# Order of the down-projection and the plan of weight rounding in a fused attention and feed-forward kernel

## The chip, the cores and the metric

The kernel runs on one core of a Trainium2 chip. The metric is the device time of one execution in microseconds (us), lower is better. The core has a matmul engine (TensorE, PE in the profile; PEld are its weight loads), a vector engine (VectorE, DVE), a scalar engine (ScalarE, ACT), GpSimd (POOL) and SyncE (SP), which issues most of the transfers. Each engine works through its own list of instructions.

## The reference, cut to what matters

Clustered attention feeds a feed-forward block. A query attends only to those keys that were given the same cluster code (16 clusters, the code is the argmax of the similarity to normalised centroids).

```python
q_assign = argmax(einsum(q_n, c_n)); k_assign = argmax(einsum(k_n, c_n))
scores = where(q_assign == k_assign, q @ k.T / sqrt(64), -1e9)
attn = softmax(scores)
x = (attn @ v), heads side by side        # (4 * 768, 8 * 64)
h = x @ w_in                              # (3072, 2048)
g = h - tanh(h)
out = g @ w_out                           # (3072, 512)
```

There are 4 batches, 8 heads, 768 tokens and a head size of 64. The feed-forward weights come as 64-bit floats.

## The kernel before

**Attention.** Two heads at a time make a pair; a batch has 4 pairs (`HP`), so there are 16. A pair's work is cut into steps: two halves of the queries (384 tokens each, `TB`), and in each half three steps (`NS`) of two key blocks. `steps` is the list of all of them; the first 12 (`HALF`) are the first half of the queries of pairs 0 to 3, the next 12 their second half, and then the pairs follow one by one. In every step a Python loop records, in this order:

- the stage `similar` (L319) of a later pair, if it is due
- `begin` of the next step: the score matmuls (L419, `sc`), and for the first halves of pairs 1 to 3 the masking matmuls with the one-hot tile `hot` (L430); then ScalarE's exponential (L441)
- `rest_of` of up to two of the weight pieces that the step is to round (L140, ScalarE)
- `value` of this step: the matmuls with v (L473) into `av`, of which there is one accumulator; in masked halves also the sums (L482, `den`)
- at the end of a half `take`, ScalarE's copy of `av` to `xT` (L492), which frees the accumulator
- the filling items of the step (the feed-forward of the batch before), and between them `todo`: the selects of the next step (L451, VectorE), `one_hot` (L394, L398), `publish` (the codes: L364, the cast `qc` of L368, a transfer to memory), `spread_both` (the broadcast load of `hot`, L386), `route` (L338 to L345), the chain that inverts the softmax sums (`total` L505, `compact` L522, `invert` L528, `spread_out` L535, `scale` L541; or `divide` L546, L549), and the rounding of the pieces.

The order on each engine is the order in which the loop records, so an instruction that waits holds up what is recorded behind it on its engine.

**Rounding.** The 64-bit weights are cut into 32 pieces of 512 KB, 16 of `w_in` and then 16 of `w_out`, each in the order of quarters 0, 2, 1, 3 (`ORDER`). A piece is loaded into one of three buffers `raw` (L193, issued by GpSimd). ScalarE turns the low words into `rest` (two buffers, L140), and VectorE makes the rounded value with three instructions (L145, L149, L152). Only when a piece is done is the load of the third next one issued (`AHEAD` = 3). Two pieces are rounded before the loop; `paces` says how many each step takes after that. Between one step and the next nothing else paces them.

**Filling.** In steps 12 to 23 the items of `plain_items(0)` fill TensorE: 16 items `up` (h = x @ w_in, L568; tanh on ScalarE, L573; g = h - tanh on VectorE, L575), then 12 items `project` (L584). A `project` item adds one quarter of `w_out` (four pieces) to the output of one block of 128 tokens; a half has three blocks (`HCH`) and four quarters (`NQ4`). The finished block is copied by ScalarE (L592) into a tile that shares its buffers with `rest`, and stored by GpSimd's queue (L593). `plain_items(1)` fills steps 24 to 47; from the second batch on another algorithm with seven products (L758, L806) takes over. The tiles `h`, `o`, `sim`, `pr`, `pq` and `den` in the accumulator memory share one pool of three buffers (`ps_f`); the scores have two buffers (`ps_s`).

Of the kernel before, what the change touches and what calls it, by code (L numbers as in the profile page):

```python
# [57 lines left out]
def kernel(  # L58
# [24 lines left out]
    HCH = NCH // 2  # L83
    NQ4 = 4
# [69 lines left out]
    def fast():  # L154
# [402 lines left out]
        def plain_items(half: int):  # L557
            gs, acc = {}, {}
            sequence = [i * FQ + o for i in ORDER for o in range(FQ)]

            def up(f: int, between):
                i, o = f // FQ, f % FQ
                if f < CF // 2:
                    gs[f] = gp.tile([P, 2, TB], F32, name="g")
                h = ps_f.tile([P, TB], F32, name="h", tag="f")
                for c in range(CD):
                    for r in halves:
                        nc.tensor.matmul(  # L568
                            h[r], lhsT=w_in[i][:, c, o * P : (o + 1) * P][:, r], rhs=xT[c][:, half],
                            start=(c == 0), stop=(c == CD - 1),  # L570
                        )
                th = thp.tile([P, TB], F32, name="th")
                nc.scalar.activation(out=th, in_=h, func=ACT.Tanh)  # L573
                between()
                nc.vector.tensor_tensor(  # L575
                    out=gs[f % HF][:, f // HF], in0=h, in1=th, op=ALU.subtract
                )

            def project(sub: int, i: int, between):
                if i == 0:  # L580
                    acc[sub] = ps_f.tile([P, DM], F32, name="o", tag="f")
                for f in sequence[i * FQ : (i + 1) * FQ]:
                    for r in halves:
                        nc.tensor.matmul(  # L584
                            acc[sub][r], lhsT=gs[f % HF][:, f // HF, sub * P : (sub + 1) * P][:, r],
                            rhs=w_out[f // FQ][:, f % FQ],
                            start=(f == sequence[0]), stop=(f == sequence[-1]),
                        )
                between()
                if i == NQ4 - 1:  # L590
                    osb = restp.tile([P, DM], F32, name="osb", tag="rest")
                    nc.scalar.copy(out=osb, in_=acc.pop(sub))  # L592
                    nc.gpsimd.dma_start(out_r[0, half * HCH + sub], osb)  # L593


            return [(2.6, 1, lambda between, f=f: up(f, between)) for f in sequence] + [
                (3.4, 1, lambda between, s=s, i=i: project(s, i, between))
                for s in range(HCH) for i in range(NQ4)
            ]


# [249 lines left out]
        NS = NCH // 2  # L851
        HALF = HP * NS
# [116 lines left out]


        fills = {HALF: (lambda: plain_items(0), HALF), 2 * HALF: (lambda: plain_items(1), 2 * HALF)}
        for b in range(1, B - 1):
            fills[2 * (b + 1) * HALF] = (lambda b=b: strassen_items(b), 2 * HALF)


        paces = {at: 1 + at % 2 for at in range(NS, HALF)}
        paces.update({at: 3 if 13 < at < 17 else 2 for at in range(HALF, HALF + 7)})
        late, divides, makers, later = [], [], [], {}
        fill, whole, spent, since, over = [], 0.0, 0.0, 0, 1
        for at, (n, half, s) in enumerate(steps):  # L980
# [72 lines left out]
            def between():  # L1053
                i = next(place)
                for it in todo[i * len(todo) // slots : (i + 1) * len(todo) // slots]:
                    it()

                if i == turned_at and 0 in stages:
                    stages[0]()
# [190 lines left out]
    with ExitStack() as cx, tc.manual_schedule():  # L1250
        fast()
# [35 lines left out]
```

## Time and profile before

| | |
|---|---|
| time, median of 3 | 1020.6 us (1019.93 to 1020.68) |
| profiled span | 1017.8 us, mean granted TensorE clock 0.996 |
| PE busy | 989.5 us (97%) |
| DVE busy | 553.0 us (54%) |
| ACT busy | 297.6 us (29%) |
| POOL busy | 500.1 us (49%) |
| h matmuls, L568 | 512 records, 488 ns in the mean |
| o matmuls, L584 | 384 records, 593 ns in the mean |
| loads of raw pieces | 16 + 16 of 512 KB, 4.9 and 4.5 us to landing in the median |

A row of a timeline gives the start in us, the length in us, the engine, the line, the operation, the tile written and those read, their sizes, and the number of instructions merged. The bracket at its end tells how long the engine was idle before it and what released it. Matmul records overlap, and a float32 matmul leaves two records, so the length of a merged row divided by its number is what one record adds to the time. One item `up` is 16 records, one item `project` too.

### The profile page before, as it was taken

What the parts mean: (1) busy time and instruction counts of PE and PEld (TensorE: products, weight loads), DVE (VectorE), ACT (ScalarE), POOL (GpSimd) and SP (SyncE); (2) the same over time, 40 slices, a digit from 0 to 9 for tenths busy, and PEclk for the clock granted to TensorE, in tenths of its full rate; (3) what the DMA queues carried; (4) which work ended last, traced back from release to release, by engine and by line L of the source; (5) the groups of instructions that cost most, each with busy time, mean ns of one, the idle gap of its engine ahead of it and who ended that gap; (6) DMA issues with size and microseconds to landing.
All of it is one profiled execution on the core that took longest, in us unless ns stands there. A gap on an engine that the chain in (4) does not pass through costs nothing.

```text
span 1017.8 us, 16547 instructions
## 1 busy us (share of the span) xinstructions
PE 989.5 (97%) x6444; PEld 471.4 (46%) x6444; DVE 553.0 (54%) x1047; ACT 297.6 (29%) x458; POOL 500.1 (49%) x343
## 2 busy tenths in 40 slices
PE   8998898999999999999999999999999999999997
PEld 4433343334443334444455555444445555344665
DVE  6468895446675657656545347755645336544011
ACT  4453443223333323332331212233332221122000
POOL 1013443345434455666678244566679345465600
PEclk9998999999999999999999999999999999999999
DMA  7654452022744834344455556344442332333321
GB/s 219 172 148 145 134 164 74 31 57 70 188 140 129 264 119 130 114 138 139 155 160 176 162 153 174 128 163 120 145 161 79 110 107 66 106 109 116 109 94 39
DMA packets 115681, 132.46 MB, mean 130 GB/s; under 512 B 62688, under 2 KB 95372, under 8 KB 112908
## 3 DMA queue, kind: packets, MB, share of 16 engines
q1 hardware_dynamic: 109212, 109.80, 35.4%
q0 software_dynamic: 6240, 21.50, 6.3%
q8 instruction: 53, 0.87, 0.4%
q14 instruction: 32, 0.26, 0.1%
q10 hardware_dynamic: 144, 0.03, 0.0%
HBM read 110.14 MB, written 21.17 MB: 129 GB/s over the span
## 4 chain that ended last, share of the span: by engine, by line
PE 86%; DVE 7%; DMA 3%; ACT 1%; issue 1%; POOL 1%; SPq 0%; ACTq 0%; DVEq 0%; POOLq 0%
PE pd L806 20%; PE pu L758 20%; PE sc L419 13%; PE av L473 12%; PE o L584 8%; PE h L568 5%; PE sim L319 2%; DMA raw<-in_moe_w_out_dram 2%; PE den L501 2%; PE pt L300 2%; DVE e L451 1%; PE den L482 1%; PE warm L270 1%; ACT t L307 1%; POOL G L749 1%
## 5 line engine op out<-in xcount | busy, mean ns | idle before, releaser
L464 POOL TENSOR_TENSOR sum<-sum,e 128x768 f32<-128x768 f32 x112 | 207.0, 1848 | 116.3 <-DVE e L451 112.5
L451 DVE SCALAR_TENSOR_TENSOR e<-row,code,sc 128x384 f32<-128x384 bf16 x336 | 185.2, 607 | 102.2 <-ACT sc L441 84.6
L806 PE MATMUL pd<-stream,G 128*64 128x256 f32 x1728 | 192.4, 380 | 2.4 <-POOL G L749 2.4
L441 ACT ACTIVATE sc<-sc 128x768 f32<-128x768 f32 x168 | 125.9, 792 | 208.6 <-PE sc L419 207.0
L806 PEld LDWEIGHTS pd<-stream,G 128*64 128x64 f32 x1728 | 123.5, 137 | 70.5 <-issue 8.0
L419 PE MATMUL sc<-t,t 64*128 64x384 f32 x768 | 151.6, 513 | 4.6 <-DVE e L451 3.9
L473 PE MATMUL av<-e,vals 128*64 128x384 f32 x768 | 147.3, 503 | 0.9 <-DVE e L451 0.9
L749 POOL TENSOR_TENSOR G<-G,th 128x768 f32<-128x768 f32 x48 | 87.4, 1834 | 104.8 <-ACT th L748 104.8
L758 PE MATMUL pu<-xT,stream 128*64 128x384 f32 x768 | 134.6, 487 | 0.7 <-DVE top L340 0.7
L758 PE MATMUL pu<-diff,stream 128*64 128x384 f32 x576 | 103.6, 488 | 1.9 <-DVE u L744 1.5
L419 PEld LDWEIGHTS sc<-t,t 64*128 64x128 f32 x768 | 66.5, 187 | 78.1 <-issue 40.3
L568 PE MATMUL h<-xT,w_in 128*64 128x384 f32 x512 | 86.4, 488 | 4.7 <-DVE g L575 4.7
L460 POOL TENSOR_TENSOR sum<-e 128x768 f32<-128x768 f32 x28 | 56.7, 2025 | 68.5 <-DVE e L451 60.5
L473 PEld LDWEIGHTS av<-e,vals 128*64 128x64 f32 x768 | 47.3, 137 | 86.4 <-issue 82.2
L758 PEld LDWEIGHTS pu<-xT,stream 128*64 128x64 f32 x768 | 54.6, 137 | 68.4 <-issue 61.7
L584 PE MATMUL o<-w_out,g 128*64 128x512 f32 x384 | 85.9, 593 | 0.0
L748 ACT ACTIVATE th<-G 128x768 f32<-128x768 f32 x48 | 40.3, 843 | 123.2 <-DVE G L744 119.6
L758 PEld LDWEIGHTS pu<-diff,stream 128*64 128x64 f32 x576 | 40.6, 137 | 52.4 <-issue 44.3
L744 DVE TENSOR_TENSOR G<-pu,u 128x384 f32<-128x384 f32 x72 | 39.7, 552 | 40.8 <-PE pu L758 40.5
L568 PEld LDWEIGHTS h<-xT,w_in 128*64 128x64 f32 x512 | 36.8, 138 | 51.4 <-issue 45.1
L584 PEld LDWEIGHTS o<-w_out,g 128*64 128x64 f32 x384 | 27.4, 137 | 50.1 <-issue 50.0
L817 DVE TENSOR_TENSOR c<-pd,du 128x256 f32<-128x256 f32 x36 | 15.1, 419 | 62.9 <-PE pd L806 62.9
(121 smaller groups left out, 850.0 us busy)
## 6 DMA issues: line engine op xcount, KB each, us to landing
stream<-up_factors SPq DMA_DIRECT2D x24, 896.0 KB
stream<-down_factors SPq DMA_DIRECT2D x21, 1024.0 KB
raw<-in_moe_w_in_dram POOLq DMA_DIRECT2D x16, 512.0 KB, 4.9
raw<-in_moe_w_out_dram POOLq DMA_DIRECT2D x16, 512.0 KB, 4.5
again<-in_moe_w_in_dram SPq DMA_DIRECT2D x32, 256.0 KB
again<-in_moe_w_out_dram SPq DMA_DIRECT2D x32, 256.0 KB
x<-in_q_dram SPq DMA_DIRECT2D x32, 192.0 KB
x<-in_k_dram SPq DMA_DIRECT2D x32, 192.0 KB
```

Source lines behind the costliest of these rows:

```text
L419: nc.tensor.matmul(sc[i][:, h, 0:TB], lhsT=turned[n, 1][r].rearrange("p a n -> p (a n)")[:, j * P : (j + 1) * P], rhs=turned[n, 0][r, half ...
L441: nc.scalar.activation(out=out, in_=sc[i][:, :, 0:TB], func=ACT.Exp, scale=SCALE)
L451: nc.vector.scalar_tensor_tensor(out=e[:, h], in0=rows[n, half][:, h], scalar=codes[n][:, 1, j // HCH, h, j % HCH : j % HCH + 1], in1=sc[: ...
L460: nc.gpsimd.tensor_tensor(out=s, in0=pair[0], in1=pair[1], op=ALU.add)
L464: nc.gpsimd.tensor_tensor(out=s, in0=s, in1=pair[i], op=ALU.add)
L473: nc.tensor.matmul(avs[n, half][h * D : h * D + D], lhsT=vals[n][:, h, j], rhs=e[i][:, h], start=(j == 0), stop=(j == NCH - 1),)
L568: nc.tensor.matmul(h[r], lhsT=w_in[i][:, c, o * P : (o + 1) * P][:, r], rhs=xT[c][:, half], start=(c == 0), stop=(c == CD - 1),)
L584: nc.tensor.matmul(acc[sub][r], lhsT=gs[f % HF][:, f // HF, sub * P : (sub + 1) * P][:, r], rhs=w_out[f // FQ][:, f % FQ], start=(f == seq ...
L748: nc.scalar.activation(out=th, in_=g[:, f], func=ACT.Tanh)
L749: nc.gpsimd.tensor_tensor(out=g[:, f].rearrange("p a n -> p (a n)"), in0=g[:, f].rearrange("p a n -> p (a n)"), in1=th.rearrange("p a n -> ...
L758: nc.tensor.matmul(ps[r], lhsT=streams[base + i][:, c, k_, r], rhs=right[c], start=(c == 0), stop=(c == CH - 1),)
L806: nc.tensor.matmul(ps[r], lhsT=left(i)[:, r], rhs=t[:, i], start=(i == 0), stop=(i == HF - 1))
```

## The change

The first half's down-projection handles two token blocks in turn: each quarter of `w_out` is applied to block 0 and to block 1 before the next quarter is begun, and the third block follows as before. The second half (`plain_items(1)`) keeps its order. With this order the later quarters of `w_out` are first used later. The plan of rounding is rewritten to go with it: it runs until step 20 instead of step 18, and it leaves out step 5, in which the codes of the last pair of the batch are published, and step 11.

```diff
+            order = [(s, i) for s in range(HCH) for i in range(NQ4)]
+            if half == 0:
+
+                order = [(s, i) for i in range(NQ4) for s in range(2)] + order[2 * NQ4 :]
             return [(2.6, 1, lambda between, f=f: up(f, between)) for f in sequence] + [
-                (3.4, 1, lambda between, s=s, i=i: project(s, i, between))
-                for s in range(HCH) for i in range(NQ4)
+                (3.4, 1, lambda between, s=s, i=i: project(s, i, between)) for s, i in order
             ]
...
-        paces = {at: 1 + at % 2 for at in range(NS, HALF)}
-        paces.update({at: 3 if 13 < at < 17 else 2 for at in range(HALF, HALF + 7)})
+
+        paces = dict(enumerate((0, 0, 0, 2, 2, 0, 1, 2, 2, 1, 1, 0, 2, 2, 2, 2, 2, 2, 2, 3, 2)))
```

Written out, the pieces of steps 3 to 20 are:

```
step    3  4  5  6  7  8  9 10 11 12 13 14 15 16 17 18 19 20
before  2  1  2  1  2  1  2  1  2  2  2  3  3  3  2  1  -  -
after   2  2  0  1  2  2  1  1  0  2  2  2  2  2  2  2  3  2
```

(Before, the plan has two pieces for step 18, of which one is left.)

## The prediction

> **What bounds the kernel now.** I read the busy time by stage first, then TensorE's timeline, then those of the engines named as releasers. The stages (cut at TensorE's first instruction of steps 12, 18 and 24; columns PE, PEld, DVE, ACT, POOL busy, TensorE clock, DMA share, GB/s):
>
> ```profile
> 39.00:88.77 49.77, 44.70 (x273) 19.28 (x273) 32.28 (x57) 25.51 (x39) 9.56 (x14) 0.99 0.57 165
> 88.77:159.79 71.02, 65.35 (x373) 28.02 (x373) 58.78 (x96) 29.15 (x51) 30.98 (x28) 0.96 0.44 137
> 159.79:226.90 67.11, 67.11 (x348) 24.70 (x348) 30.54 (x49) 17.73 (x27) 24.79 (x17) 1.00 0.18 47
> 226.90:1017.80 790.90, 778.19 (x5277) 380.78 (x5273) 407.52 (x772) 209.25 (x318) 430.94 (x272) 1.00 0.42 131
> ```
>
> From 160 us on TensorE never rests for long: what is gained before stays gained. In steps 12 to 17 (second line) VectorE is busy 83%, and the clock is below 1; in 18 to 23 it is busy 46%. TensorE's timeline shows the losses:
>
> ```profile
> 65.70 1.56 PE L419 MATMUL sc<-t,t 64*128 64x384 f32 x8
> 68.78 0.50 PE L430 MATMUL sc<-hot 64*128 64x384 bf16 x4 [1.52 <-DVE hot L398]
> ...
> 81.50 1.61 PE L419 MATMUL sc<-t,t 64*128 64x384 f32 x8 [0.39 <-ACT e L441]
> ...
> 88.77 2.93 PE L419 MATMUL sc<-t,t 64*128 64x384 f32 x8 [2.93 <-DVE e L451]
> ...
> 104.36 0.92 PE L419 MATMUL sc<-t,t 64*128 64x384 f32 x4 [0.99 <-DVE e L451]
> ...
> 122.73 2.80 PE L568 MATMUL h<-xT,w_in 128*64 128x384 f32 x16 [2.12 <-DVE g L575]
> ...
> 157.06 2.80 PE L568 MATMUL h<-xT,w_in 128*64 128x384 f32 x16 [2.57 <-DVE g L575]
> ```
>
> After the idle 2.93 us the same eight matmuls take 2.93 instead of 1.56 us: in windows of 1 us the granted clock is 0.50 from 88.2 to 95.0, so 6.8 us at half speed, 3.4 us lost. Sum: 1.5 + 0.4 + 2.9 + 3.4 + 1.0 + 2.1 + 2.6 = 13.9 us. That is the ceiling of any gain here.
>
> Why VectorE is late (its timeline): it stands still for the last codes (`hot` of pair 3), then works off a queue of pieces (1.9 us each: 0.42 + 0.69 + 0.69 and gaps), so that the selects of step 12 come at 87.49.
>
> ```profile
> 56.72 0.28 DVE L368 CAST qc<-pq 24x128 bf16<-24x128 f32 x1 [0.46 <-PE pq L364]
> ...
> 68.08 0.42 DVE L394 TENSOR_SCALAR hot<-hot,mine_code 128x768 bf16<-128x768 bf16 x1 [5.40 <-DMA den<-back]
> ...
> 70.45 0.19 DVE L528 RECIPROCAL each<-each 128x6 f32<-128x6 f32 x1 [0.53 <-DMA each<-list]
> ...
> 87.49 2.18 DVE L451 SCALAR_TENSOR_TENSOR e<-row,code,sc 128x384 f32<-128x384 bf16 x4
> ```
>
> ScalarE, in its order, has `rest` (first part of a rounding) ahead of the copy L492 that frees the only `av` accumulator, and of the tanh that `g` needs:
>
> ```profile
> 72.54 0.68 ACT L140 ACTIVATE rest<-raw 128x512 uint32<-128x512 uint32 x1 [1.87 <-DVE w_in L152]
> 73.11 0.47 ACT L492 COPY xT<-av 128x384 f32<-128x384 f32 x1
> ...
> 155.00 0.66 ACT L140 ACTIVATE rest<-raw 128x512 uint32<-128x512 uint32 x1 [3.02 <-DMA raw<-in_moe_w_out_dram]
> ```
>
> The last of these, a wait for a transfer, is what the 2.57 us at 157.06 come from.
>
> **What the Trainium skill says.** "TensorE: Matmul & The Clock Gate" (What's actually happening): the clock falls to half after an idle window of about 3.4 us and returns after a busy one, the window running freely. The trace agrees (two such windows low), though 2.93 us idle sufficed. The same page (Architectural detail) calls ScalarE and VectorE strict FIFO; the trace agrees, tanh L573 at 155.9 follows that `rest`. "DMA: Bandwidth & Descriptors" (Issuing engines are not separate DMA queues): all queues share 16 DMA engines; here raw, `hot` and `den` share 243 GB/s from 62 to 68.5. "SBUF — State Buffer" (SBUF: two separate sides): VectorE and GpSimd lock a port pair; here an L145 beside a GpSimd sum took 1.86 instead of 0.42 us (104.59).
>
> **The change part by part.** Piece numbers count from 0; 16 to 31 are w_out. No piece's work changes.
>
> *Rounding.* Pieces done after steps 4, 5, 7, 8, 11, 12, 17, 18, 19, 20: before 5, 7, 10, 11, 16, 18, 31, 32; after 6, 6, 9, 11, 13, 15, 25, 27, 30, 32.
>
> (a) Step 4 has one piece more ahead of the cast `qc`, step 5 none. The cast comes 1.4 us later (56.2 + 1.9 = 58.1). Before, raw 8, 9 and 10 were asked for at 58.6 to 62.4, beside `hot`; after, raw 10 waits for piece 7, behind `hot`. From 62 on: before 2 raw (1.05 MB) + hot 0.39 + den 0.20; after one raw, 1.1 MB in all, at 243 to 280 GB/s 4.0 to 4.5 us from 62.7. Estimate: `hot` at 67.0 instead of 68.0, `each` at 68.7 instead of 70.4. The 1.5 us wait at 67.2 goes (bounds: 0.5 us longer to gone).
>
> (b) A new wait. Raw 10 is now asked for only once piece 7 is read: 68.7 + 1.3 + 0.5 (issue) = 70.5; landing takes 4.7 us in the median (3.7 to 7.3 in this stretch); I take 4.5: 75.0. Its `rest` now stands at the head of step 8 (before, step 8 had one piece, fetched at 62.4). Behind it on ScalarE: L492, den L505, the exponentials of step 10. L492 ends at 75.0 + 0.6 + 0.5 = 76.1. TensorE, which reaches the first av of step 9 at 72.3 (73.8 before), waits for it: 3.8 us idle, 2.3 us later than before. Bounds: 3.7 and 5.1 us of landing (the latter is raw 11's, issued 72.22, used 77.35) give 75.3 and 76.7.
>
> (c) The clock. An idle 3.8 us should halve it as 2.93 us did: 3.4 us (bounds 0 and 3.4). The work from there to step 12: av + den 2.73, then 4.55, then 4.22 = 11.5 us. Step 12 begins at 76.1 + 11.5 + 3.4 = 91.0. VectorE's list up to the selects of step 12 is as long as before (six pieces after `hot`), but GpSimd's `wholes` waits for the late L505; I get the selects at 89 to 91, just hidden. So step 12 starts 2.2 us later than the 88.77 of before, with the clock already up.
>
> (d) Steps 12 to 17. TensorE's work: 16 up items x 2.58 + 6 x 2.93 (sc, av) + 2 den x 0.65 + transposes 1.46 = 61.6 us, 10.3 a step. VectorE a step: selects 2.2, g 1.4, two pieces 3.8, port locks about 1.4 = 8.8 (before: 2.8 pieces, 10.9). No pieces stand between the selects of steps 12 and 13 now (before two, 3.9 us), and raws are asked for over 10 us ahead of most needs, so the waits 0.99, 2.12 and 2.57 go. The first up needs xT of pair 3, whose reciprocals (2.6 us, after GpSimd) come 0.6 us late; I leave 1.0 us for single late raws. 61.6 + 0.6 + 1.0 = 63.2; step 18 at 154.2 instead of 159.8: 5.6 us gained.
>
> *Steps 18 to 20 and the order of the projections.* Seven pieces move in here (2 + 3 + 2, against 1). TensorE has 2.93 + 6.87 = 9.8 us a step. Step 19 is VectorE's fullest: 2.2 + route 2.3 + 0.8 + 3 x 1.9 = 11.0, with locks 12 to 13; step 18 and 20 about 7. Quarter 2 of w_out is complete with the first piece of step 19, about 12 us into it, and needed 15.8 us in; the last piece about 23 us in, needed at 26. The side-by-side order makes this possible: two blocks use a quarter before the next is asked for, and the number of matmuls (384 of 593 ns recorded) is the same. Both accumulators take two of three buffers of that pool; the third serves pr, den and pq, a step apart each. The osb copies come together in step 21, after the last rest. All hidden: 0.
>
> Sum: 1020.6 - 5.6 = 1015.0 us.
>
> **The rivals.** (1) The clock does not fall, the idle time straddling two windows, or raw 10 lands early: step 12 at 87.7, gain 8.9, 1011.7. For: the idle 2.57 us before 157.06 did not lower it. Against: the gap is longer than the 2.93 us that did. (2) The codes come no sooner than before and raw 10 lands late: av of step 9 at 78.4, step 12 at 93.3, step 18 at 156.5; gain 3.3, 1017.3. For: piece 5 does delay the cast. (3) Slower: the projections wait. With one buffer for pr, den and pq behind a loaded VectorE, three waits of about 2.5 us (route's 2.3 us and an eviction), 7.5 us against 5.6 gained: 1022.5. For: step 19's 12 to 13 us against 9.8; against: step 18 leaves slack, and each wait needs TensorE to be ahead. (4) Both cancel: 1020.6.
>
> **How the numbers follow.** Forecast 0.44, rival 1 0.25, rival 2 0.17, rival 3 0.10, rival 4 0.04. Faster by over 0.2% (2 us): the first three, 0.86; same 0.04; slower 0.10. The range takes in rivals 1 and 2 and their bounds: from 1010.0 (landing 3.7 us with the clock up) to 1019.0.
>
> **What would show it.** Right: the wait before sc<-hot at about 67 gone; an idle 3 to 4 us before av in step 9, released by L492, with a `rest` that waited for raw 10; half clock then and none at 88 to 95; step 18's first matmul at 154; no wait of the projections on w_out. Wrong: an idle TensorE between 154 and 222, no gap at 73 to 76, or g L575 still holding h in steps 14 and 17.

## The result and the profile after

The changed kernel takes 1012.4 us in the median of four runs (1010.4 to 1013.1), against 1020.6 us (1019.9 to 1021.2) for the kernel before: 0.9917 of it, 95% interval 0.9899 to 0.9934. Beside the later experiments, on another chip, it was run again: 1012.4 against 1019.4 us, 0.9928 (0.9912 to 0.9945). It is faster, by 7 to 8 us.

The busy time by stage, cut at the same instructions as before (the last cut of before, at 226.90, lies 0.2 us behind its row at 226.71; columns PE, PEld, DVE, ACT, POOL busy, TensorE clock, DMA share, GB/s):

```profile
39.00:90.55 51.55, 46.14 (x272) 19.80 (x272) 30.32 (x55) 24.46 (x38) 9.45 (x13) 0.97 0.56 159
90.55:152.60 62.05, 62.00 (x375) 27.13 (x373) 49.68 (x80) 27.30 (x46) 29.17 (x25) 1.00 0.34 110
152.60:219.67 67.07, 67.07 (x346) 24.44 (x346) 41.55 (x64) 21.41 (x33) 28.18 (x22) 1.00 0.30 91
219.67:1010.80 791.13, 778.38 (x5279) 380.69 (x5275) 406.22 (x773) 209.62 (x318) 432.18 (x272) 1.00 0.42 131
```

Compare the lengths (second column) with those of before. The first stage is 1.8 us longer, steps 12 to 17 are 9.0 us shorter (62.05 instead of 71.02), and the two after that are unchanged within 0.3 us. VectorE's work has moved from the second stage (58.8 to 49.7 us) to the third (30.5 to 41.6 us), where it costs nothing. So there are two effects of opposite sign. TensorE's timeline shows both:

```profile
65.58 1.56 PE L419 MATMUL sc<-t,t 64*128 64x384 f32 x8
68.49 0.50 PE L430 MATMUL sc<-hot 64*128 64x384 bf16 x4 [1.35 <-DVE hot L398]
...
73.04 0.49 PE L430 MATMUL sc<-hot 64*128 64x384 bf16 x4
77.36 2.55 PE L473 MATMUL av<-e,vals 128*64 128x384 f32 x8 [3.83 <-ACT xT L492]
...
90.55 1.56 PE L419 MATMUL sc<-t,t 64*128 64x384 f32 x8
...
123.74 7.91 PE L568 MATMUL h<-xT,w_in 128*64 128x384 f32 x48
...
149.87 2.80 PE L568 MATMUL h<-xT,w_in 128*64 128x384 f32 x16
152.60 0.85 PE L319 MATMUL sim<-t,bd 128*32 128x384 f32 x8
```

From 90.55 to 222 us no row of this timeline has a bracket: the waits of 0.99, 2.12 and 2.57 us are gone. The wait for `hot` is nearly what it was (1.35 against 1.52 us). New is the wait of 3.83 us before `av` in step 9, released by the copy L492. ScalarE's timeline shows why that copy is late, GpSimd's why the piece ahead of it is:

```profile
71.00 0.70 ACT L140 ACTIVATE rest<-raw 128x512 uint32<-128x512 uint32 x1 [0.63 <-DVE w_in L152]
76.27 0.67 ACT L140 ACTIVATE rest<-raw 128x512 uint32<-128x512 uint32 x1 [4.56 <-DMA raw<-in_moe_w_in_dram]
76.84 0.46 ACT L492 COPY xT<-av 128x384 f32<-128x384 f32 x1
```

```profile
60.68 0.53 POOL L193 DMA_DIRECT2D raw<-in_moe_w_in_dram  x1 [2.01 <-ACT rest L140]
70.69 0.74 POOL L193 DMA_DIRECT2D raw<-in_moe_w_in_dram  x1 [9.48 <-ACT e L441]
```

```profile
69.45 0.69 DVE L149 SCALAR_TENSOR_TENSOR w_in<-raw,w_in 128x512 uint32<-128x512 uint32 x1
```

Raw 10 is issued at 70.69, ten microseconds after the one before it, because its buffer is read by piece 7, which stands behind `hot` on VectorE (last row). The bracket names an exponential of ScalarE, which doesn't touch the buffer; piece 7's L149, which reads it last, ends at 70.14, 0.55 us before the issue. In the kernel before, piece 7 ran ahead of `hot`, and raw 10 was issued at 62.39. Now raw 10 is used at 76.2, and ScalarE has meanwhile waited 4.56 us with L492 behind it. Two windows of 1 us from the clock's drop and its return:

```profile
77.00:78.00 1.00, 0.64 (x4) 0.42 (x6) 0.86 (x2) 1.00 (x3) 0.21 (x1) 0.84 0.71 291
...
81.00:82.00 1.00, 1.00 (x8) 0.40 (x6) 0.97 (x2) 0.00 (x0) 0.18 (x1) 0.95 0.86 299
```

The third column from the right is the granted clock. Between the two it is 0.50: about 3.4 us at half speed in all, 1.7 us lost, half of what the kernel before loses at 88 to 95 us. (I call such a stretch a half clock.)

With this the two profiles, 1017.8 and 1010.8 us long, can be reconciled. The three waits that are gone give 5.7 us, and the shorter half clock gives 1.7. The pauses up to step 12 take back 0.3 (1.35 and 3.83 us, against 1.52, 0.39 and 2.93). That makes 7.1 us, against 7.0 between the spans (the medians are 8.2 us apart). The half clock of before lies in the second stage, the new one in the first; so the second stage shows 9.0 us and the first a loss.

The landmarks that the experiments are read by are two starts on TensorE: the first matmuls that step 12 records (scores), and the first of step 18 (`sim`, L319). Before: 88.77 and 159.79. Changed: 90.55 and 152.60.

### The profile page after: what moved, and what is told of

It reads as the page before. It is cut to its first block, busy times and chain, and to the rows that moved or that the text cites. A ratio compares the mean times of both kernels' runs of the same rounds, so it can differ in the third digit from the quotient of the medians.

```text
span 1010.8 us, 16557 instructions
## 1 busy us (share of the span) xinstructions
PE 987.7 (98%) x6444; PEld 470.6 (47%) x6444; DVE 551.7 (55%) x1047; ACT 298.8 (30%) x458; POOL 502.8 (50%) x343
## 4 chain that ended last, share of the span: by engine, by line
PE 91%; DVE 3%; DMA 1%; ACT 1%; POOL 1%; issue 1%; SPq 0%; DVEq 0%; ACTq 0%; POOLq 0%
PE pd L809 20%; PE pu L761 20%; PE sc L419 13%; PE av L473 13%; PE o L584 8%; PE h L568 8%; PE sim L319 2%; PE den L501 2%; PE pt L300 2%; PE den L482 1%; PE warm L270 1%; ACT t L307 1%; POOL G L752 1%; PE pr L332 1%; DMA hot<-q_codes 1%
## 5 line engine op out<-in xcount | busy, mean ns | idle before, releaser
L809 PEld LDWEIGHTS pd<-stream,G 128*64 128x64 f32 x1728 | 123.5, 137 | 70.5 <-issue 8.0
L419 PEld LDWEIGHTS sc<-t,t 64*128 64x128 f32 x768 | 66.0, 186 | 73.6 <-issue 41.6
```

The lines of the kernel that those rows point to most:

```text
L419: nc.tensor.matmul(sc[i][:, h, 0:TB], lhsT=turned[n, 1][r].rearrange("p a n -> p (a n)")[:, j * P : (j + 1) * P], rhs=turned[n, 0][r, half ...
L809: nc.tensor.matmul(ps[r], lhsT=left(i)[:, r], rhs=t[:, i], start=(i == 0), stop=(i == HF - 1))
```

## The experiments

The first four ran together on one chip, beside a kernel before of 1018.6 us (23 runs, 1017.0 to 1021.5); the last four together on another, beside one of 1019.4 us (7 runs, 1019.1 to 1020.7). Plans are the pieces of steps 3 to 20. The edits are shown against the changed kernel, that of experiment 2 against the kernel before. Landmarks and waits are those of one profiled run each.

**1. The order alone.**

```diff
-        paces = dict(enumerate((0, 0, 0, 2, 2, 0, 1, 2, 2, 1, 1, 0, 2, 2, 2, 2, 2, 2, 2, 3, 2)))
+        paces = {at: 1 + at % 2 for at in range(NS, HALF)}
+        paces.update({at: 3 if 13 < at < 17 else 2 for at in range(HALF, HALF + 7)})
```

> The side-by-side order of the projections alone, with the plan of rounding of before. My theory: the order by itself moves no wait, it only permits later rounding; the losses of the kernel before (idle 1.5, 0.4, 2.9, 1.0, 2.1, 2.6 us and 3.4 us of half clock) all stay, step 18 starts at 159.8 us: 1020.6 us, within 1 us. Rival (the order itself saves time on TensorE or in the evictions): 1 us or more below 1020.6, and a step 18 to 23 shorter than 67.1 us.

Measured: 1019.5 us, ratio 1.0012 (1.0003 to 1.0020). Step 18 starts at 159.49, and from there to step 24 it takes 63.3 us, as before (223.09 - 159.79). The old waits are there in other sizes: 2.70, 1.74, 0.65 and 2.74 us instead of 2.93, 0.99, 2.12 and 2.57. The clock falls twice for 3.4 us each, at 103.7 and, in the last wait, at 154.9:

```profile
87.44 1.97 PE L419 MATMUL sc<-t,t 64*128 64x384 f32 x8 [2.70 <-DVE e L451]
...
102.15 0.92 PE L419 MATMUL sc<-t,t 64*128 64x384 f32 x4 [1.74 <-DVE e L451]
...
155.24 4.31 PE L568 MATMUL h<-xT,w_in 128*64 128x384 f32 x16 [2.74 <-DVE g L575]
```

The order by itself gains nothing (the interval even has it 0.03 to 0.2% slower). What it is good for follows from the code: with the old order, block 0 would use the third and fourth quarter of `w_out` in step 19, ahead of pieces that the new plan rounds in steps 19 and 20. That pairing was not run.

**2. The early part of the plan alone,** with the order of before: 2, 2, 0, 1, 2, 2, 1, 1, 0, then 2, 3, 3, 3, 3, 3, 2. The pieces that the early part leaves over must then go into steps 12 to 18, so steps 12 to 17 have 17 (before 15, changed 12).

```diff
-        paces = {at: 1 + at % 2 for at in range(NS, HALF)}
-        paces.update({at: 3 if 13 < at < 17 else 2 for at in range(HALF, HALF + 7)})
+        paces = dict(enumerate((0, 0, 0, 2, 2, 0, 1, 2, 2, 1, 1, 0, 2, 3, 3, 3, 3, 3, 2)))
```

> The order of before, the changed plan up to step 11 (no pieces in steps 5 and 11), and the rest packed into steps 12 to 18 (2, 3, 3, 3, 3, 3, 2). My theory: up to step 12 as in the changed kernel (new wait 3.8 us before av of step 9, step 12's score matmuls at about 90.5 us), then a VectorE with 2.8 pieces a step as before: waits of h for g of 2 to 5 us in steps 12 to 17, step 18 at 154.6 to 158: 1015.5 to 1019. Rival (the gain is from the early plan alone, the late steps had room): step 18 at 153, 1012.5 us.

Measured: 1016.8 us in 12 runs (1013.4 to 1019.2), ratio 0.9983 (0.9971 to 0.9995). Step 12 starts at 89.98, step 18 at 155.38, so 65.4 us lie between, 3.3 more than in the changed kernel. Two waits make up 3.1 of them:

```profile
76.79 2.33 PE L473 MATMUL av<-e,vals 128*64 128x384 f32 x8 [3.97 <-ACT xT L492]
...
118.81 2.80 PE L568 MATMUL h<-xT,w_in 128*64 128x384 f32 x16 [0.98 <-DVE g L575]
...
152.65 2.80 PE L568 MATMUL h<-xT,w_in 128*64 128x384 f32 x16 [2.08 <-DVE g L575]
```

The early part brings the new wait with it, and without relief in steps 12 to 17 the waits of h for g come back. Taken alone, with its surplus of late pieces, it is worth 1.7 us (0.0017 of 1018.6).

**3. The late part alone:** the plan of before through step 11, then 1, 1, 2, 2, 2, 1, 2, 3, 2, with the new order. Three pieces more are done early than in the changed kernel, so steps 12 to 17 have 9 instead of 12: the late part is lighter here.

```diff
-        paces = dict(enumerate((0, 0, 0, 2, 2, 0, 1, 2, 2, 1, 1, 0, 2, 2, 2, 2, 2, 2, 2, 3, 2)))
+        paces = dict(enumerate((0, 0, 0, 2, 1, 2, 1, 2, 1, 2, 1, 2, 1, 1, 2, 2, 2, 1, 2, 3, 2)))
```

> The changed order and the late end of the rounding, with the plan of before through step 11; steps 12 to 20 take 1, 1, 2, 2, 2, 1, 2, 3, 2 pieces. My theory: no new wait in step 9, but the idle 2.9 us before step 12's score matmuls, the half clock behind it (3.4 us) and about 1 us before step 13 stay; the waits of 2.1 and 2.6 us go: step 18 at 154.8, 1015.6 us. Rival (late relief brings nothing, all comes from the codes): 1019.5 us or more. If this plan is better than the changed one early on, under 1012 us.

Measured: 1012.1 us, ratio 0.9938 (0.9922 to 0.9955). Step 12 starts at 87.80 after a wait of 2.26 us, with 1.7 us lost to a half clock behind it; step 18 starts at 151.79. Not one wait is left between.

```profile
87.80 2.06 PE L419 MATMUL sc<-t,t 64*128 64x384 f32 x8 [2.26 <-DVE e L451]
...
151.79 0.85 PE L319 MATMUL sim<-t,bd 128*32 128x384 f32 x8
```

This run has all the gain of the changed kernel within the noise (0.9928 in its second measurement), without the pause for the codes. I expected 154.8 for step 18: this run lost half of the clock time that I had copied from the profile of before, and the wait before step 13 went too. There are still two pieces between the selects of steps 12 and 13, so the pieces were not its cause. With one piece in step 12 there is one `rest` less ahead of the tanh on ScalarE (before, that second `rest` waited for its transfer until 101.50), and the g between the selects no longer waits for it (99.59, without a bracket; 102.61 before).

**4. Piece 10 one step later:** steps 8 and 9 take 1 and 2 instead of 2 and 1.

```diff
-        paces = dict(enumerate((0, 0, 0, 2, 2, 0, 1, 2, 2, 1, 1, 0, 2, 2, 2, 2, 2, 2, 2, 3, 2)))
+        paces = dict(enumerate((0, 0, 0, 2, 2, 0, 1, 2, 1, 2, 1, 0, 2, 2, 2, 2, 2, 2, 2, 3, 2)))
```

> The changed kernel with piece 10 moved from step 8 to step 9 (steps 8 and 9 take 1 and 2 instead of 2 and 1), so that its rest is recorded behind the copy L492 that frees the av accumulator. My theory: the 3.8 us wait before av of step 9 goes, and the half clock (1.6 us) with it; VectorE's list up to the selects of step 12 is as long as ever, so TensorE waits there for 0 to 1.5 us: step 12 at about 86.5 instead of 90.6, 1008.5 us. Rival (the wait only moves on, to VectorE's selects and with a half clock as before): 1011 to 1013 us.

Measured: 1010.6 us, ratio 0.9928 (0.9911 to 0.9944); I expected 1008.5, the rival 1011 to 1013. The wait before `av` is gone. Step 12 starts at 86.43, as expected, but the rival was half right too: TensorE now stops there instead, and the clock falls (from 87.6 to 91.0, 1.7 us lost).

```profile
67.78 0.50 PE L430 MATMUL sc<-hot 64*128 64x384 bf16 x4 [0.79 <-DVE hot L398]
86.43 2.63 PE L419 MATMUL sc<-t,t 64*128 64x384 f32 x8 [2.10 <-DVE e L451]
```

VectorE's list says why. From `hot` on it has six pieces and the reciprocals to do before the selects of step 12, and in the changed kernel the wait before `av` had hidden that:

```profile
67.08 0.42 DVE L394 TENSOR_SCALAR hot<-hot,mine_code 128x768 bf16<-128x768 bf16 x1 [6.12 <-DMA hot<-q_codes]
...
85.15 2.18 DVE L451 SCALAR_TENSOR_TENSOR e<-row,code,sc 128x384 f32<-128x384 bf16 x4
```

**5. The changed kernel again,** beside the next three.

> The changed kernel once more, beside the next three on one chip: 0.990 to 0.994 of the kernel before, the 3.8 us wait before av of step 9, a half clock behind it of 1.6 to 3.4 us.

Measured: 1012.4 us, 0.9928; the wait before `av` is 3.58 us, 1.7 us are lost to the clock, and the landmarks are 89.54 and 151.58. The wait for `hot` is 0.82 us here.

```profile
76.35 2.05 PE L473 MATMUL av<-e,vals 128*64 128x384 f32 x8 [3.58 <-ACT xT L492]
```

**6. Only the order on ScalarE:** the same pieces in the same steps, but the `rest` of piece 10 behind the copy L492.

```diff
-            for piece in todays[:2]:
+            for piece in todays[: 1 if at == 8 else 2]:
                 rest_of(piece)
             value(n, half, s)
             if s == NS - 1:
                 take(n, half)
+            if at == 8:
+                rest_of(todays[1])
+            if s == NS - 1:
```

> The changed kernel, the same pieces in the same steps; only the rest of piece 10 is recorded behind the copy L492 of step 8 instead of ahead of it. My theory (ScalarE's order makes the wait, not the amount of rounding): av of step 9 starts at about 73.5 without a wait; rest 10 still waits for its transfer until about 76.2 and holds the exponential of step 10, so TensorE waits about 1.5 us before the score matmuls of step 10 or 11; no half clock; step 12 at 87 to 88.5 instead of 90.6: 2 to 4 us below the changed kernel. Rival (the accumulator is held by something else): the wait of 3.8 us before av stays.

Measured: 1010.5 us, ratio 0.9910 (0.9894 to 0.9927), 2 us below the changed kernel beside it. TensorE starts `av` of step 9 without a wait; what is left of the loss sits where expected, in the exponential of step 10 that the same `rest` now delays:

```profile
73.09 1.51 PE L473 MATMUL av<-e,vals 128*64 128x384 f32 x8
...
77.92 1.62 PE L419 MATMUL sc<-t,t 64*128 64x384 f32 x8 [2.03 <-ACT e L441]
...
88.14 1.97 PE L419 MATMUL sc<-t,t 64*128 64x384 f32 x8 [1.32 <-DVE e L451]
```

Nothing but the place of one 0.7 us instruction was changed, so the wait of 3.6 to 3.8 us before `av` was ScalarE's order, not the amount of rounding. But the idle time moved rather than shrank: 1.57, 2.03 and 1.32 us up to step 12, against 0.82 and 3.58 us in the run of experiment 5. What the profiled run gains up to step 12 (88.14 against 89.54) is the half clock: the idle time, now in smaller parts, does not lower the clock (1.00 from 70 to 95 us). Other runs of this kernel had mean clocks of 0.996 to 0.999, so it may fall in some of them.

**7. Five pieces between the codes and the selects:** steps 8 to 11 take 1, 2, 0, 0, step 18 takes 3.

```diff
-        paces = dict(enumerate((0, 0, 0, 2, 2, 0, 1, 2, 2, 1, 1, 0, 2, 2, 2, 2, 2, 2, 2, 3, 2)))
+        paces = dict(enumerate((0, 0, 0, 2, 2, 0, 1, 2, 1, 2, 0, 0, 2, 2, 2, 2, 2, 2, 3, 3, 2)))
```

> Steps 8 to 11 take 1, 2, 0, 0 pieces (in the run before this one 1, 2, 1, 0; in the changed kernel 2, 1, 1, 0), and step 18 three. My theory: with five instead of six pieces between hot and the selects of step 12 VectorE reaches these 1.9 us earlier, at about 83.3, and the 2.1 us wait before step 12's score matmuls and the 1.7 us of half clock go: step 12 at 84.3, step 18 at 146.5, ratio to the kernel before 0.989 (3.9 us below the run with six). Rival (the wait goes elsewhere, to w_out in steps 18 to 20 or to h in 12 to 17): ratio 0.992 or more.

Measured: 1007.9 us, ratio 0.9885 (0.9868 to 0.9901). The run "before this one" of the expectation is experiment 4. The wait before step 12 is down to 1.06 us, with the clock up; step 12 starts at 85.63, step 18 at 147.81. It is 1.3 us later than expected, since the selects came at 84.35 instead of 83.3: this run's VectorE waited until 69.2 for the sums' transfer (L528; 68.1 in experiment 4).

**8. The codes first:** as 7, with one piece in step 4 and three in step 17.

```diff
-        paces = dict(enumerate((0, 0, 0, 2, 2, 0, 1, 2, 2, 1, 1, 0, 2, 2, 2, 2, 2, 2, 2, 3, 2)))
+        paces = dict(enumerate((0, 0, 0, 2, 1, 0, 1, 2, 1, 2, 0, 0, 2, 2, 2, 2, 2, 3, 3, 3, 2)))
```

> As the run before, and step 4 takes one piece instead of two, so that the cast of the last codes (qc) is not held up; step 17 takes three. Steps 3 to 20: 2, 1, 0, 1, 2, 1, 2, 0, 0, 2, 2, 2, 2, 2, 3, 3, 3, 2. My theory: the cast at about 56.8 instead of 57.9, hot 1 us earlier, the wait of 0.8 to 1.4 us before its matmuls gone: about 1 us below the run before, ratio 0.988. Rival (hot is bound by the transfers, not by the cast): no difference to the run before within 0.5 us.

Measured: 1007.2 us, ratio 0.9876 (0.9860 to 0.9893), the fastest here. The two waits that remain are short:

```profile
68.03 0.50 PE L430 MATMUL sc<-hot 64*128 64x384 bf16 x4 [0.34 <-DVE hot L398]
...
85.09 1.97 PE L419 MATMUL sc<-t,t 64*128 64x384 f32 x8 [0.52 <-DVE e L451]
```

The wait for the codes fell from 1.43 (experiment 7) to 0.34 us, as expected. But the profiled run was 1.15 us late at step 7 already (61.59 against 60.44 for the score matmuls), and `hot` came no sooner on the clock of the profile (67.33 against 67.27). Counted from the matmul that delivers the codes (`pq`, at 56.83 and 55.68), it came 1.1 us sooner. The wait differs by 0.8 us between runs that have the same early plan (0.79 in experiment 4, 1.57 in 6), and the intervals of 7 and 8 overlap. That the piece ahead of the cast costs about 1 us is likely, not shown.

## Why the prediction was right

The time was forecast at 1015.0 us and measured at 1012.4; in the two profiles step 18 starts 7.2 us earlier, against 5.6 forecast. The mechanism held, but for the wait for the codes, which was to go and stayed; the sizes of four terms were off, and their errors partly cancelled.

- (a) The codes. The cast did come later (57.94, forecast 58.1). The load of `hot` then took 6.7 us from its issue (L386) to its use, against 7.8 before, with fewer raw loads beside it, but was issued 0.8 us later (61.12 against 60.28). So `hot` came at 67.79, not at 67.0, and the wait became 1.35 instead of 1.52 us. In experiment 5 the same kernel had it at 67.02, as forecast, and still waited 0.82 us. The working has a slip here: the matmul starts 0.70 us after `hot` does (68.08 and 68.78 before), so a `hot` that is 1.0 us sooner shortens a wait of 1.5 us and does not remove it.
- (b) The new wait. Raw 10 was issued at 70.69 (forecast 70.5) and took 5.5 us to use instead of 4.5. TensorE stood still for 3.83 us where 3.8 were forecast. That the length agrees is luck: the wait began 1.2 us late (73.5 instead of 72.3), because of (a), and ended 1.3 us late, because of the transfer. Its mechanism is no luck: experiment 6 shows that ScalarE's order is the cause, and 4 that moving the piece removes it.
- (c) The clock. It fell, but for about 3.4 instead of 6.8 us: 1.7 us lost against 3.4. This is the mis-sized term that counts most. It made up for (a) and (b): step 12 started at 90.55, forecast 91.0. The forecast copied the 3.4 us from a single fall; what sets the length is in the last section, and the forecast could not have known it.
- (d) Steps 12 to 17 took 62.05 us, forecast 63.2. Of the 1.6 us set aside for the sums of pair 3 and single late raws nothing was used: TensorE was busy for 62.00 of the 62.05 us, and the work itself came to 0.4 us more than the 61.6 of the sum. All three old waits went, as said; experiments 1 and 3 show that the later rounding does this. For the 0.99 us wait I had named the pieces between the selects of steps 12 and 13; experiment 3 points to the second `rest` of step 12.
- Steps 18 to 20 cost nothing, as forecast: from `sim` of step 18 to `sim` of step 24 it takes 63.46 us against 63.30. The margin is thin, as computed: the last piece is done 23.4 us after step 19 begins at 163.18 (forecast 23) and needed at 26.3:

```profile
185.36 1.27 DVE L152 CUSTOM_DVE_ANT_0 w_out<-w_out,rest 128x1024 uint16<-128x1024 uint16 x1
```

```profile
186.88 3.60 PE L584 MATMUL o<-w_out,g 128*64 128x512 f32 x16
```

  VectorE ends it at 186.6, 0.3 us before the first matmul of the last quarter; the piece's own matmuls are the last of those 16 records, some 2.6 us on.

Of the rivals, the first named the time best (1011.7 us), but not by its cause: the clock did fall. The two causes of the second came half true in this profile (`hot` only 0.3 us sooner than before, raw 10 a microsecond late: `av` of step 9 at 77.36, between its 78.4 and the forecast's 76.1); its time, 1017.3, did not, because (c) and (d) fell short. The third (waits of the projections) is refuted; no such wait is in the trace.

What the prediction did not see is how the two halves of the plan weigh. A late part alone, lighter by three pieces, has the whole gain (experiment 3); the early part of the plan adds to it only once its new wait is out of the way. With piece 10 moved and one piece less after the codes, 4.5 to 5.2 us more are to be had (experiments 7 and 8 against 5).

## What to carry to other kernels

When one engine's list is too full in one stage and half empty in the next, moving work across costs nothing if the reader's order can be changed so that it needs the result later; count the load of each stage on that engine first. When a plan paces several engines at once, follow the load that each item triggers. Piece 10 stayed in step 8; but piece 7, whose buffer it loads into, moved from step 6 to step 7 and so behind `hot`, and the transfer was asked for 8.3 us later (70.69 instead of 62.39). The first instruction of piece 10 then waited in an in-order list ahead of a copy that frees the only accumulator. After removing such a wait look at once for the next engine's list that it had hidden.

## What the runs showed of the hardware

TensorE's clock did not follow the length of the pause. After pauses of 2.93 us (before), 3.83 us (changed), 2.26 us (experiment 3) and 2.10 us (experiment 4) it fell to half. After pauses of 2.57 us (before, at 157 us), 2.03 us (experiment 6) and 2.70 us (experiment 1, at 87 us) it did not, while in experiment 1 it fell at 103.7 us, 1.6 us after a pause of 1.74 us.

It followed a grid of 3.41 us. Within a trace, falls and returns lie a whole number of these stretches apart: before, 88.15 and 94.98; in experiment 1, 103.72, 107.13, 154.92 and 158.33, where from the first to the third it is 15 stretches of 3.413 us. Cut along the grid, the kernel before looks like this (the clock is third from the right):

```profile
84.74:88.15 3.41, 1.10 (x8) 0.26 (x4) 3.24 (x7) 1.37 (x3) 1.06 (x2) 1.00 0.79 247
88.15:91.57 3.42, 2.80 (x8) 1.23 (x8) 1.52 (x3) 1.78 (x4) 0.28 (x1) 0.50 0.61 190
91.57:94.98 3.41, 3.41 (x14) 1.33 (x14) 2.62 (x4) 1.03 (x2) 2.48 (x2) 0.50 0.03 6
...
153.01:156.42 3.41, 1.48 (x14) 1.24 (x12) 0.23 (x1) 1.43 (x4) 1.81 (x1) 1.00 0.56 216
```

The clock fell at the end of a stretch in which TensorE had done little: it was busy for 1.10 us of it here, 0.32 in the changed kernel and 0.83 in its second run, 0.54, 1.61 and 1.18 in experiments 2, 3 and 4, 1.68 and 1.00 in experiment 1. So no stretch had to be idle throughout. Pauses without a fall left about as much as the largest of these or more: 1.48 us here (the grid cuts the pause before 157.06 in two) and 1.74 at 118.87, 1.49 in experiment 1 at 83.24, 1.51 in experiment 6. The end of the program aside, every stretch with less than 1.2 us was followed by a fall. Between 1.48 and 1.74 us both happened, and what decides there is open; the busy times are rough, since the ends of matmuls are modelled.

The return goes by the same grid. In seven of the eight falls TensorE was busy for 3.09 to 3.42 us of the stretch that followed, and the clock came back at its end. In the kernel before, the pause reached 0.6 us over the edge, 2.80 us were busy, and the clock stayed low for a second stretch. So one fall costs 1.7 or 3.4 us.

The grid lies differently against the program in each trace (an edge is at 88.15 before and at 89.54 in experiment 3), so the same pause can cost 0, 1.7 or 3.4 us. Runs of one kernel do differ in the clock: in experiment 2 the mean granted clock of a run goes from 0.995 to 0.999, and its two shortest runs, 1013.4 and 1014.1 us, are those at 0.999. That the place of the grid makes this difference is likely, not shown.
